# A new written-out order of 1,051 operations for a gated linear attention followed by a token and channel mixer

## The chip, the cores and the metric

One core of a Trainium2 chip. The metric is the time of one execution in device microseconds (us), lower is better. The kernel before took 176.54 us (median of 3 runs, 176.35 to 176.94).

## The reference

Four batches, 8 heads, 768 steps, 48 columns a head. An attention with a decaying state is computed first, and its output, 384 columns wide, goes through a two-part mixer:

```
f = 1 / (1 + exp(-f_logit))
for t in range(S):
    state = f[t] * state + outer(k[t], v[t])
    y[t]  = q[t] @ state
x  = y, heads side by side                      # 4 x 768 x 384
u  = x + (relu(x.T @ w_tok1) @ w_tok2).T        # mixes the 768 steps, through 256
out = u + relu(u @ w_ch1) @ w_ch2               # mixes the 384 columns, through 1536
```

## The kernel before

Everything runs in bf16 matmuls with float32 sums. The 768 steps of a batch are six chunks of 128. The kernel first builds a plan: some 1,051 small operations, each with a number in the order in which it was added, the engines that may run it, what it needs and makes, and the PSUM bank that it fills. `Plan.run` then issues them in the order of a list written out by hand of a program, `ORDER`. A token of the list is an operation's number; a letter after it (A, D, G) chooses ScalarE, VectorE or GpSimd where there is a choice; digits after colons are the PSUM banks (eight of them) that it takes; `z11` and `s18` at the head are idle matmuls of 512 and of 64 columns that only keep TensorE running. Every engine works through its own part of the list strictly in order and waits on semaphores for what an operation needs, so the list sets what each engine does next, but no times. GpSimd issues the loads, SyncE issues the stores, small copies and the transposes done by DMA, each in the list's order.

Operations are named here by kind, batch, chunk (or part). Those that the text speaks of:

- load,f / load,q / load,k / load,v (line 266, GpSimd; the first three of f on SyncE) and the loads of weights (line 272). For batch 0 a load brings two chunks, later one chunk; f of batches 1 to 3 comes in one load.
- gates: exp and ln of f on ScalarE (lines 371, 372; 388, 392 for batch 0), and lo (lines 379, 401), the low bf16 half of the logarithm, on VectorE or GpSimd.
- sums (lines 461, 462; 615, 618): a triangular matmul that adds the logarithms up along a chunk. G and Gi (lines 471, 473; 628, 630) are its exponentials, and gated (lines 490, 637) multiplies q and k by them on VectorE. grow and glast (lines 477, 481) bring the decay of a whole chunk to all partitions, by a small DMA from SyncE.
- turn: q and k of a chunk are transposed, by matmul and a copy (turned) in batches 0 to 2, by a DMA transpose from SyncE (line 503) in batch 3. The transposed chunk goes into one of two buffers, chunk number modulo 2, so that turn,3,3 must wait until y,3,1 has read its buffer.
- scores (lines 413, 676), masked (lines 541, 706, VectorE), parts (lines 429, 665: the chunk's share of the state), tsum, state and spread (the state's step and its copy into bf16, on VectorE, GpSimd and ScalarE), y (lines 560, 564, 743; within for pairs of batch 0, line 719) and its copies x_bf and x_nat.
- tok1, h1T, tok2, u, u_bf: the mixer over steps (tok1 is line 757, tok2 line 773, u line 789). ut transposes u: by matmul with a copy uT (line 811) in batches 0 and 1, by two DMA transposes (line 802) in batches 2 and 3, where ut,2,0 carries chunks 0 to 2 and ut,2,1 chunks 3 to 5.
- ch1 (line 826), zT (lines 357, 359), ch2 (line 845), sum (line 851, VectorE) and store (line 855, SyncE): the mixer over columns. ch1 and ch2 are over half of TensorE's time. ch1,b,th,cc is one of 24 pieces a batch, th the half of the steps; ch2,b,tt,0,k0 is a third of the sum of chunk tt.

The list weaves the batches into each other: while TensorE works on the mixer of batch b, the gates, sums, scores and states of batch b+1 are fed in between. In batch 0 the attention runs alone at the start, with chunks taken in pairs.

In the plan each operation carries a cost (`kind`). `run` does not read it; such costs serve the program that made the list.

## Time and profile before

| what | value |
|---|---|
| median of the runs shown | 176.54 us |
| the profiled execution | 175.49 us, with a span of 173.6 us from its first to its last instruction |
| TensorE busy | 162.2 us, 93% of the span |
| VectorE, ScalarE, GpSimd busy | 127.7, 101.4 and 92.6 us |
| moved from and to memory | 25.17 MB read, 4.72 MB written |
| loads issued by GpSimd | 56, those of 96 KB landing 5.1 (v) to 7.4 us (k) after their issue at the median, those of 1152 KB after 9.9 |
| DMA transposes | 6 of q and k, 4 of u, 3.3 and 2.9 us to landing at the median |

The page of the profile shows one execution. Its busy rows give how long each engine worked; a chain of waits, followed back from the last instruction, tells what set the end; timelines of one engine list its instructions in order of time, merged when they follow each other, with the idle time ahead of them in brackets and what ended it. "issue" there means that the engine waited for nothing that the profile shows. Matmuls overlap each other, so a row of 12 matmuls of 384 columns with a mean of 326 ns lasts far less than 12 times that.

### The profile page before, as it was taken

The numbers are of one execution on the slowest core, as the hardware profiler recorded it, in microseconds if no ns is written. First come the engines' busy times: TensorE is split into PE (matmuls) and PEld (weight loads), VectorE is DVE, ScalarE is ACT, GpSimd is POOL, SyncE is SP. The second block draws the span as 40 slices with busy tenths as digits, with TensorE's granted clock in tenths as the row PEclk, the third lists the DMA queues.
The fourth block names the chain that finished last, engine by engine and source line by source line (L and its number), as shares of the span: only waits on it lengthen the run. The fifth ranks groups of instructions, "written<-read, shape, count | busy, mean of one in ns | idle before, by whom it ended". The sixth has DMA issues, their size and how long they took to land.

```text
span 173.6 us, 4462 instructions
## 1 busy us (share of the span) xinstructions
PE 162.2 (93%) x1761; PEld 103.6 (60%) x1761; DVE 127.7 (74%) x272; ACT 101.4 (58%) x226; POOL 92.6 (53%) x135
## 2 busy tenths in 40 slices
PE   6998779999999999899999999896999999999990
PEld 2575655666566666566767665563656556656660
DVE  5778988969969857887999779895884804766141
ACT  3899896986681448799999547478457120032000
POOL 8999979994996998794983707321110020000000
PEclk9999978999999999999999999999999999999999
DMA  5999999999999999169999992967530151030075
GB/s 152 227 171 195 206 196 188 185 149 203 146 177 201 102 69 88 5 65 228 121 95 144 120 59 51 210 169 240 134 66 4 47 135 46 4 136 0 30 263 211
DMA packets 89573, 22.74 MB, mean 131 GB/s; under 512 B 82288, under 2 KB 88736, under 8 KB 89552
## 3 DMA queue, kind: packets, MB, share of 16 engines
q0 software_dynamic: 69600, 13.77, 91.2%
q1 hardware_dynamic: 19952, 8.69, 18.9%
q8 instruction: 14, 0.23, 0.6%
q14 instruction: 7, 0.06, 0.1%
HBM read 25.17 MB, written 4.72 MB: 172 GB/s over the span
## 4 chain that ended last, share of the span: by engine, by line
PE 83%; DVE 6%; DMA 5%; issue 3%; ACT 2%; DVEq 0%; ACTq 0%
PE ps L826 26%; PE ps L845 23%; PE ps L757 5%; DMA qkT<-qk 5%; PE ps L773 4%; PE ps L877 3%; PE ps L500 3%; PE ps L618 2%; PE ps L413 2%; PE ps L461 2%; PE ps L564 2%; PE ps L462 2%; PE ps L560 1%; DVE AmT L541 1%; PE ps L644 1%
## 5 line engine op out<-in xcount | busy, mean ns | idle before, releaser
L826 PE MATMUL ps<-uT,w_ch 128*128 128x384 bf16 x288 | 53.0, 326 | 0.1
L845 PE MATMUL ps<-w_ch,zT 128*128 128x384 bf16 (+2 forms) x300 | 52.6, 320 | 0.0
L845 PEld LDWEIGHTS <-zT 128*128 128x128 bf16 x300 | 28.2, 98 | 17.3
L826 PEld LDWEIGHTS <-w_ch 128*128 128x128 bf16 x288 | 27.2, 97 | 17.1 <-issue 0.3
L357 ACT ACTIVATE zT<-ps 128x384 bf16<-128x384 f32 x50 | 22.6, 496 | 24.8 <-DVE zT L359 12.6
L359 DVE TENSOR_SCALAR zT<-ps 128x384 bf16<-128x384 f32 x46 | 23.8, 549 | 6.9 <-PE ps L826 6.7
L851 DVE TENSOR_TENSOR x_nat<-x_nat,ps 128x384 f32<-128x384 f32 (+2 forms) x25 | 12.9, 530 | 16.2 <-PE ps L845 16.2
L541 DVE TENSOR_TENSOR AmT<-ps,tri_bf 128x512 bf16<-128x512 f32 x36 | 23.1, 682 | 2.0 <-PE ps L413 2.0
L266 POOL DMA_DIRECT2D v_sb<-in_v_dram x16 | 15.7, 984 | 3.4 <-DVE zT L359 3.4
L281 POOL CAST state_bd<-state 48x192 bf16<-48x192 f32 x27 | 9.2, 341 | 13.5 <-DVE state L549 4.3
L266 POOL DMA_DIRECT2D qk_sb<-in_q_dram x16 | 16.0, 1001 | 0.3 <-issue 0.2
L266 POOL DMA_DIRECT2D qk_sb<-in_k_dram x16 | 15.7, 990 | 0.1
L281 POOL CAST u_bf<-x_nat 128x384 bf16<-128x384 f32 x14 | 7.5, 548 | 14.5 <-issue 11.8
L789 DVE TENSOR_TENSOR x_nat<-x_nat,ps 128x384 f32<-128x384 f32 x21 | 10.8, 545 | 2.7 <-PE ps L773 2.6
L379 POOL TENSOR_TENSOR Llo<-L 128x384 bf16<-128x384 f32 x11 | 9.0, 825 | 6.4 <-ACT L L372 6.2
L757 PE MATMUL ps<-x_bf,w_tok 128*128 128x384 bf16 x48 | 12.0, 339 | 0.0
L490 DVE TENSOR_TENSOR qk<-qk_sb,GG 128x768 bf16<-128x768 bf16 x18 | 10.8, 620 | 0.7 <-DMA qkT<-qk 0.7
L277 ACT ACTIVATE x_bf<-ps 128x384 bf16<-128x384 f32 x14 | 6.9, 491 | 6.2 <-PE ps L564 6.2
L473 ACT ACTIVATE GG<-ps 128x384 bf16<-128x384 f32 x18 | 8.8, 497 | 2.3 <-PE ps L462 2.2
L471 ACT ACTIVATE GG<-ps 128x384 bf16<-128x384 f32 x18 | 8.6, 505 | 1.4 <-PE ps L462 0.9
L773 PE MATMUL ps<-h1T,w_tok 128*128 128x384 bf16 x48 | 9.3, 326 | 0.0
L577 POOL TENSOR_TENSOR state<-tsum,glast 128x192 f32<-128x192 f32 x9 | 4.7, 523 | 8.3 <-ACT state_bd L277 6.7
(100 smaller groups left out, 265.7 us busy)
## 6 DMA issues: line engine op xcount, KB each, us to landing
out_dram<-x_nat SPq DMA_DIRECT2D x23, 192.0 KB, 2.2
f_sb<-in_f_logit_dram POOLq DMA_DIRECT2D x3, 1152.0 KB, 9.9
f_sb<-in_f_logit_dram SPq DMA_DIRECT2D x3, 384.0 KB, 4.0
qk_sb<-in_q_dram POOLq DMA_DIRECT2D x12, 96.0 KB, 5.6
qk_sb<-in_k_dram POOLq DMA_DIRECT2D x12, 96.0 KB, 7.4
w_ch<-in_moe_w_ch_dram POOLq DMA_DIRECT2D x2, 576.0 KB, 9.3
v_sb<-in_v_dram POOLq DMA_DIRECT2D x12, 96.0 KB, 5.1
w_ch<-in_moe_w_ch_dram POOLq DMA_DIRECT2D x1, 1152.0 KB, 10.6
```

The costliest lines, as they stand in the source:

```text
L266: lambda eng=eng, into=into, of=of: eng.dma_start(out=into, in_=of),
L281: nc.gpsimd.tensor_copy(out_, in_)
L357: nc.scalar.activation(out_, in_, AF.Relu, bias=0.0, scale=1.0)
L359: nc.vector.tensor_scalar(out_, in_, 0.0, None, ALU.max)
L490: add(("gated", b, c, *names), DVE, lambda n=n: nc.vector.tensor_tensor(qk[it][:, n, :, 0:D], qk_sb[nb][:, n, :, c, :], GG[i][:, n], ALU.m ...
L541: add(("masked", b, c, p), DVE, lambda half=half, made=made: nc.vector.tensor_tensor(half, made(), tb4, ALU.mult), need=["tri_bf"], make=[ ...
L757: add(("tok1", b, rt, kt), PE, lambda rt=rt, kt=kt, pm=pm: nc.tensor.matmul(banks[pm.at][:, 0:DM], lhsT=w_tok1[:, kt, rt * 128:(rt + 1) * ...
L773: nc.tensor.matmul(banks[pm.at][:, 0:DM], lhsT=w_tok2[:, kt, tt * 128:(tt + 1) * 128], rhs=h1T[:, kt, :], start=(kt == 0 and not held), st ...
L789: nc.vector.tensor_tensor(to, un, banks[pm.at][:, 0:DM], ALU.add)
L826: nc.tensor.matmul(banks[pm.at][:, 0:384].rearrange("p (n t) -> p n t", t=128), lhsT=w[:, kt, c0:c0 + 128], rhs=uT[:, rows3, kt, :], start ...
L845: nc.tensor.matmul(banks[pm.at][:, 0:n1 - n0], lhsT=zT[:, kt, tt * 128:(tt + 1) * 128], rhs=w_ch2[:, kt, n0:n1], start=(kt == 0), stop=(kt ...
L851: add(("sum", b, tt, n0), DVE, lambda un=un, pm=pm, n=n1 - n0: nc.vector.tensor_tensor(un, un, banks[pm.at][:, 0:n], ALU.add), make=[("x_n ...
```

## The change

`ORDER` is replaced as a whole; nothing else in the file differs. It is a permutation of the same 1,051 operations with other choices of engine and of banks, and with ten idle matmuls of 512 columns and 22 of 64 at its head instead of eleven and 18.

```diff
 ORDER = """
-z11 s18 14D 6D 7G 8G 32 21G 9G 12D 33 0G 5G 1 10G 2 49 51 50 20G 15D 3D 17D 23D 24D 26D 27D 36 54 34 55 35 37 29D 18D 38
-22D 28 25D 53G 39 52D 19D 58 11G 13D 105:0 106 107 40 57D 56D 100:1 137:2 41 142:3 109 30D 102 101 103 108 59 111:0 104
...
+z10 s22 0G 20G 5G 7D 14G 6D 19D 21D 22G 1 13G 23A 2 26A 32 33 25G 8G 11D 34 3A 49 17D 28 35 36 51 53D 50 54 52D 55 24D
+15G 37 12G 39 105:0 58 9D 27D 16D 38 100:1 18D 57D 29D 30D 10G 31D 107 56G 108 106 110 109 102 142:2 101 104 103 137:0
+59 42 41 4G 40 61D 60D 114:1 119:3:4 115 111:5 144 139 145 138 112 175:0 62 143 125 113A 140 146 126G 116D 148:2 149
...
```

Told by names, what changes where the text goes on:

- The eight paired loads of batch 0 (two chunks each). Before: q,0,0 k,0,0 v,0,0 k,0,2 q,0,2 v,0,2 k,0,4 q,0,4. After: k,0,0 q,0,0 v,0,0 q,0,2 k,0,2 q,0,4 k,0,4 v,0,2. Then load,f,1 and load,v,0,4 in both.
- TensorE's opening. Before: sums of chunks 1, 0, 2, 3, the turns of chunks 0 and 1, with parts,0,0 ahead of the last, sums,0,5, ... sums,0,4, ... parts,0,2, within,0,0. After: sums 1, 0, 3, 2, turn,0,0 of k, parts,0,0, the other turns, sums,0,4, ... sums,0,5, ... parts,0,2, within,0,0. From there to within,0,2 and on to tok1 the two orders are nearly the same.
- Engines. 28 of the zT move from VectorE to ScalarE and 20 the other way. Seven lo move from GpSimd to VectorE and two the other way: 16 on VectorE and 8 on GpSimd after, 11 and 13 before. 11 spread move from ScalarE to GpSimd and 9 the other way; 7 x_bf and 7 x_nat move from ScalarE to VectorE, 5 and 3 the other way.
- Batch 3 on TensorE. Before: y,2,5, 22 operations that end with three ch2, scores,3,1, scores,3,0, parts,3,2, sums,3,4, ch1,2 (four), y,3,1, ch1,2 (six), y,3,0, sums,3,5, scores,3,2, scores,3,3. After: y,2,5, 20 operations, scores,3,0, scores,3,1, parts,3,2, two ch2, y,3,0, sums,3,5, sums,3,4, three ch2, y,3,1, ch1,2 (seven), scores,3,2, scores,3,3.
- SyncE around it. Before: glast,3,0, turn,3,0, turn,3,1, ut,2,0, ut,2,1, glast,3,2, turn,3,2, glast,3,3, store,0,3, store,0,1, turn,3,3, glast,3,4, six stores. After: glast,3,0, turn,3,1, turn,3,0, glast,3,3, glast,3,2, store,0,0, store,1,0, glast,3,1, ut,2,0, ut,2,1, store,0,1, turn,3,2, turn,3,3, store,0,2, glast,3,4.
- GpSimd in the middle. After: spread,1,0, load,f,2, load,k,2,0, load,v,2,1, lo,1,5, load,q,2,0, load,k,2,1, both halves of spread,1,1.
- The stores on SyncE at the end. Before: ... 3,3, 2,1, 1,4, 2,4, 1,0, 1,5, 3,2, the right part of 3,5, the left one, 3,1, 3,4, 3,0. After: ... 1,4, 2,4, 3,3, the right part of 3,5, 3,4, 3,2, 3,1, the left part of 3,5, 3,0, with all of batches 1 and 2 ahead of 3,3. The last seven TensorE operations are the same in both.

More of the change, by code (lines that the diff above doesn't have):

```diff
@@ new lines @@
+962G 967 994:3 1008:2 970:4 971A 977A 998:6 806 792 817 968:0 972:4 996:1 991A 802 992:5 995D 993A 1000:3 1001D 988:7
+568 563 973A 1009A 969A 1010:5 982:3 1004:0 984:2 978:4 989D 997A 1002:1 1005A 986:0 999D 983A 1012:3 573 1006:6 987D
+1011A 1003A 797 1014:0 1026:1 1036:5 979D 980:4 1046:7 807 1015A 985D 1007D 1021:0 1041:6 981A 1042 1031:4 1047 1013D
+1037 1032 1048 1049 1027 1033 1028 1043 1034 578 1016:4 812 1044 1029 1038 1022 1023 1035 1050 1039 1024 1017 1040 1018
+1030 1025 1045 1019 1020
```

76 lines of the change are left out of this document (35 added, 41 removed).

## Prediction

> **What bounds the kernel now.** I read the page first, its busy rows and the chain that ended last.
>
> ```profile
> span 173.6 us, 4462 instructions
> ...
> PE 162.2 (93%) x1761; PEld 103.6 (60%) x1761; DVE 127.7 (74%) x272; ACT 101.4 (58%) x226; POOL 92.6 (53%) x135
> ...
> q8 instruction: 14, 0.23, 0.6%
> ...
> PE 83%; DVE 6%; DMA 5%; issue 3%; ACT 2%; DVEq 0%; ACTq 0%
> ```
>
> TensorE is the bound, and the new list has the same matmuls, three more idle ones apart. So the time can only change where TensorE stands, or where its clock is low. Next I cut the span into stages (columns: length, busy time and instructions of each engine, granted clock, DMA share, GB/s).
>
> ```profile
> 7.26:23.32 16.06, 13.04 (x325) 9.60 (x322) 13.91 (x35) 14.65 (x32) 15.46 (x21) 1.00 1.60 189
> 23.32:33.66 10.34, 10.34 (x146) 7.16 (x146) 8.79 (x20) 8.53 (x20) 9.04 (x15) 0.83 1.60 192
> 33.66:111.00 77.34, 76.36 (x800) 49.32 (x797) 64.13 (x126) 55.09 (x126) 56.75 (x73) 1.00 1.55 122
> 111.00:121.00 10.00, 8.14 (x104) 5.03 (x106) 8.12 (x17) 7.39 (x18) 1.59 (x5) 1.00 0.76 197
> 121.00:169.50 48.50, 48.49 (x368) 30.06 (x366) 27.34 (x55) 11.35 (x26) 3.04 (x7) 1.00 0.28 84
> ```
>
> The first row is the opening, batch 0's attention: TensorE idles 16.06 - 13.04 = 3.0 us. It idles 1.0 in the long middle, 1.9 between 111 and 121, and nothing from there to 169.5. The second stage runs at 0.83 of the clock, which is 0.17 x 10.34 = 1.8 us of a lower clock's loss. That is all a list can win, with some 4 us at the end that no matmul fills. Dense work goes at 0.163 us a matmul of 384 columns, in the chain by time:
>
> ```profile
> 137.55 5.20 PE ps L845 x32
> ```
>
> **The transposes of batch 3.** Two entries of the chain are DMAs, and TensorE's and SyncE's timelines show what surrounds them.
>
> ```profile
> 107.69 3.28 DMA qkT<-qk
> 115.65 4.93 DMA qkT<-qk
> ```
>
> ```profile
> 108.51 2.12 PE L845 MATMUL ps<-w_ch,zT 128*128 128x384 bf16 x12
> 111.02 0.62 PE L413 MATMUL ps<-qkT 48*128 48x128 bf16 x16 [0.39 <-DMA qkT<-qk]
> ...
> 111.95 0.34 PE L461 MATMUL ps<-L,tri_bf 128*128 128x384 bf16 x1
> ...
> 112.57 2.11 PE L826 MATMUL ps<-uT,w_ch 128*128 128x384 bf16 x12
> ...
> 114.75 0.36 PE L564 MATMUL ps<-v_sb,AmT 128*128 128x48 bf16 x8
> ...
> 118.51 0.40 PE L413 MATMUL ps<-qkT 48*128 48x128 bf16 x8
> 120.63 0.40 PE L413 MATMUL ps<-qkT 48*128 48x128 bf16 x8 [1.73 <-DMA qkT<-qk]
> ```
>
> ```profile
> 112.54 1.26 SPq L503 DMA_TRANSPOSE qkT<-qk  x1
> ...
> 114.48 1.06 SPq L855 DMA_DIRECT2D out_dram<-x_nat  x2
> 115.65 1.24 SPq L503 DMA_TRANSPOSE qkT<-qk  x1
> ```
>
> Three losses, from start to start. scores,3,1 begins at 111.02, where the 12 matmuls before it end at 108.51 + 12 x 0.163 = 110.46: 0.55. sums,3,4 and the first product of ch1,2 lie 0.62 apart where two matmuls of 384 columns need 0.33: 0.29. scores,3,3 begins 2.12 after scores,3,2, whose 8 matmuls take half of the 0.55 of a 16-matmul pair: 1.8. Together 2.65.
>
> In the new list turn,3,1, which is issued first, waits for y,2,5, the last reader of its buffer. Between y,2,5 and scores,3,0 stand 49 matmuls of 384 columns, 8.0 us, against the issue of one transpose (1.26) and the transfer of the next (3.28), 4.6 us: the 0.55 goes. Late next would be gated,3,0, which has the rest, 3.4 us, as its cover. ch1,2 no longer follows sums,3,4 at once, so the 0.29 goes. turn,3,3 must wait for y,3,1 in both lists, since it overwrites that chunk's buffer. Before, y,3,1 was done at 114.75 + 0.36 = 115.11, but SyncE was issuing two stores until 115.54. After, turn,3,2 stands right ahead of turn,3,3, and one store ahead of both, so I expect the issue at y,3,1's end. Seven ch1 (21 x 0.163 = 3.42) and scores,3,2 (0.3) follow until scores,3,3: 3.7 us of cover for a transfer of 3.28, if it isn't slowed to 4.93 again. I take no wait: the 1.8 goes.
>
> SyncE issues in order, so a step that waits there holds all behind it. store,0,0,0, store,1,0,0 and glast,3,1 now stand ahead of ut,2,0 and ut,2,1. The matmuls of those two sums end over 20 operations before, so the stores only cost their issue, twice half of the 1.06 above. ut,2,1 needs u,2,5 and u_bf,2,5, some 0.55 each as a vector row further down shows, and about 3.3 for the transfer, 4.4 us. From tok2,2,5 to ch1,2,1,11, its first user, stand 24 matmuls of 384 columns (3.9 us) and the scores, parts and y of chunks 0 and 1 (0.55 for the scores alone), so about 5 us: hidden by a little, and if that cover is gone, ch1,2 and all behind it start so much later.
>
> **The opening.** Three of the loads around which the list is reordered, v,0,2, q,0,4 and f,1, as GpSimd issues them, and the views of the DMAs issued at those moments (last column: us from issue to landing):
>
> ```profile
> 8.49 0.88 POOL L266 DMA_DIRECT2D v_sb<-in_v_dram  x1
> ...
> 10.22 0.90 POOL L266 DMA_DIRECT2D qk_sb<-in_q_dram  x1
> ...
> 12.41 2.26 POOL L266 DMA_DIRECT2D f_sb<-in_f_logit_dram  x1
> ```
>
> ```profile
> v_sb<-in_v_dram POOLq DMA_DIRECT2D x1, 192.0 KB, 5.1
> ...
> qk_sb<-in_q_dram POOLq DMA_DIRECT2D x1, 192.0 KB, 6.8
> ...
> f_sb<-in_f_logit_dram POOLq DMA_DIRECT2D x1, 1152.0 KB, 9.9
> ```
>
> ```profile
> 17.12 0.24 PE L665 MATMUL ps<-v_sb,qk 64*64 64x48 bf16 x7 [0.41 <-issue]
> ...
> 22.38 0.22 PE L719 MATMUL ps<-v_sb,zT 64*128 64x48 bf16 x4 [0.57 <-ACT x_bf L277]
> 23.32 0.51 PE L719 MATMUL ps<-v_sb,zT 64*128 64x48 bf16 x27 [0.72 <-issue]
> ```
>
> TensorE stands twice inside an operation, for nothing but "issue": at the 222nd and the 350th matmul, 128 apart. A load and a matmul are two instructions, so that is each 256 instructions. Queue q8 moved 0.23 MB in 14 transfers, 16 KB each, and 2 x 1761 instructions over 14 are 252. I read these as fetches of TensorE's own instructions, late because the loads fill the DMA engines. By count of the new list the same two places fall into the same two operations, parts,0,2 and within,0,2. The second begins to wait for its block when the first is passed (17.12), and has it 6.2 us later.
>
> v,0,2 moves from the sixth to the eighth of these loads: it lands not at 13.6 but about where the eighth did, 10.22 + 6.8 = 17.0. parts,0,2 needs it and ran from 16.3, standing until 17.12: cost 0.1 while the fetch covers it. What starts earlier in the new list (one idle matmul of 512 columns fewer, four small ones more, both low parts of the first sums on VectorE) shortens what lies ahead of 17.12, where fetch and load hold TensorE anyway: I count it at nothing. So within,0,2 again goes on at 23.3, and the low clock follows, since TensorE has stood at the same places before. Bounds: 1.3 gained (0.41, and 0.94 from 22.38 to 23.32) if the fetches come sooner; 5.2 lost if v,0,2 lands only with f,1 (12.41 + 9.9 = 22.3 against 17.1); and the 1.8 of the clock, gone or doubled. I stay near the row of the eighth load.
>
> The Trainium skill ("Runtime: NRT & Kernel Launch", Instruction fetch mechanics) says that blocks of 256 instructions are fetched ahead and the crossing is mostly hidden. The block size agrees with the rows; "hidden" does not, with 0.41 and 0.72 of standing. By that rule the opening would move with its data, the fourth rival.
>
> **What VectorE gets.** Low parts (lo) on VectorE rise from 11 to 16, on GpSimd they fall from 13 to 8.
>
> ```profile
> L379 DVE TENSOR_TENSOR Llo<-L 128x384 bf16<-128x384 f32 x7 | 5.0, 721 | 0.0
> ...
> L789 DVE TENSOR_TENSOR x_nat<-x_nat,ps 128x384 f32<-128x384 f32 x21 | 10.8, 545 | 2.7 <-PE ps L773 2.6
> ```
>
> ```profile
> 68.56 1.50 DVE L379 TENSOR_TENSOR Llo<-L 128x384 bf16<-128x384 f32 x1
> ```
>
> ```profile
> 68.34 0.84 POOL L379 TENSOR_TENSOR Llo<-L 128x384 bf16<-128x384 f32 x1
> ```
>
> ```profile
> 69.41 0.49 PE L773 MATMUL ps<-h1T,w_tok 128*128 128x384 bf16 x2
> 70.37 0.33 PE L461 MATMUL ps<-L,tri_bf 128*128 128x384 bf16 x1 [0.48 <-DVE uT L279]
> ```
>
> lo,2,0 took 1.50 instead of 0.72 while GpSimd ran lo,2,1, and TensorE then lost 70.37 - 69.41 - 0.33 = 0.63. The new list has lo,2,1 on VectorE just as GpSimd has lo,2,2, so I keep this loss. The new list has tight places of its own. ut,0,4 takes the bank of tok2,0,0,1, which u_bf,0,0 and u,0,0 (0.55 each) must empty, with uT,0,2 between them (a third operation, some 0.35 as an estimate, being a shorter copy); TensorE has seven matmuls of 128 to 384 columns and turn,1,1 meanwhile, about 1.3: 0.2 lost. ch2,1,3,0,0 takes the bank of tok2,2,5 after two scores and parts, under 1.0, and u,2,5 must empty it behind two gatings and a sum: 0 to 1 lost, 0.5 taken. y,1,2 needs both halves of spread,1,1 from GpSimd, where f,2 (2.26), four loads of 0.9 and a low part (0.84) stand ahead of them, 6.7 us after state,1,0; 43 matmuls of 384 columns (7.0 us) and smaller ones cover that: nothing lost, and each us that GpSimd is behind is one at y,1,2. Five more low parts beside GpSimd cost nothing to 5 x 0.78 = 3.9; each has the sums of its chunk as its only reader, which the list puts a few operations later, so I take nothing beyond the 0.63, with 3.9 as the upper end.
>
> The Trainium skill ("SBUF — State Buffer", SBUF: two separate sides) says that a VectorE operation with two inputs in SBUF and a GpSimd operation that reads SBUF exclude each other. The 1.50 agrees. By that rule each of the five can wait out a GpSimd operation, 5 x 0.84 = 4.2 as an estimate, and the second rival would be the outcome.
>
> **The end.**
>
> ```profile
> 164.62 6.39 SPq L855 DMA_DIRECT2D out_dram<-x_nat  x10
> ```
>
> ```profile
> 169.59 0.55 DVE L851 TENSOR_TENSOR x_nat<-x_nat,ps 128x384 f32<-128x384 f32 x1 [0.35 <-PE ps L845]
> ```
>
> ```profile
> 170.60 0.41 SPq L855 DMA_DIRECT2D out_dram<-x_nat  x1
> ```
>
> The last sum is done at 170.14; its store waits 0.46 because SyncE still works off ten stores. In the new list the sums of batches 1 and 2 are all done before the first ch2 of batch 3, their stores are issued ahead of store,3,3, and the last seven TensorE operations are the same as before. So SyncE is free when the last sum is done: I take 0.4. If it is not, nothing changes here, since the 0.46 stands already.
>
> **Sum.** 0.55 + 0.29 + 1.8 + 0.4 = 3.0 gained, 0.1 + 0.2 + 0.5 = 0.8 lost, 2.2 net. The profiled execution took 175.49 (span 173.6), which gives 173.3. The runs shown have a median of 176.54, 1.05 above it, and the new kernel will be timed as they were; against that it is 176.54 - 2.2 = **174.3**.
>
> **Rivals.** 1. *turn,3,3 is slowed again.* By the count of 128 matmuls a fetch falls at y,3,0 in the old list and at scores,3,2 in the new one; if it meets the transfer, 4.93 against 3.7 leaves 1.2: 175.5. For it: nearly the same place. Against: one store behind it, not six. 2. *The low parts fill VectorE*: 2.2 of the 3.9 reach TensorE, no change: 176.5. For it: the 1.50 and the 0.63. Against: the six other low parts of that row had 5.0 - 1.5 = 3.5 us, 0.58 each, so most met no GpSimd operation. 3. *Slower: v,0,2 is late.* From 17.1 on each us of its landing is one of the total; from 17.1 + 2.2 + 0.5 = 19.8 the kernel is slower. Landing at 21 costs 3.9: 178.2. For it: the eighth load already took 6.8, and f,1 is issued right behind. Against: loads so far landed in their order. 4. *The opening isn't held by fetches*: 1.3 more, 173.0. For it: parts,0,0 has its inputs earlier. Against: the two rows with "issue".
>
> **How the numbers follow.** Forecast 0.36, slowed transpose 0.18, full VectorE 0.16, late load 0.19, free opening 0.11. A measurement here tells 0.3% (0.5 us) from no change. Faster: 0.36 + 0.18 + 0.11 = 0.65; same 0.16; slower 0.19. The range 172.3 to 177.7 leaves out the worse half of the late load, a lower clock that stays longer, and the ends of the free opening.
>
> **What would show it.** Right: no wait on qkT at scores,3,1 and scores,3,3, a last store issued within 0.1 of its sum, and issue stalls in parts,0,2 and within,0,2 with the latter going on near 23.3. Wrong: parts,0,2 waiting for v_sb after 17.2; a turn,3,3 near 5 us; new waits of TensorE on VectorE between 34 and 111.

## The result, and the profile after

The new list is slower: 178.75 us (median of 4 runs, 177.81 to 178.96) against 176.56 for the kernel before (4 runs, 176.35 to 176.94), a ratio of 1.0111, 95% interval 1.0072 to 1.0151. The forecast was 174.3, and 178.75 lies outside its range too. The profiled execution took 178.96, with a span of 177.2, 3.6 more than before.

The page of the kernel after, with the rows that answer to those of before:

```profile
span 177.2 us, 4472 instructions
...
PE 163.1 (92%) x1764; PEld 104.1 (59%) x1764; DVE 132.1 (75%) x272; ACT 102.6 (58%) x229; POOL 89.7 (51%) x132
...
q8 instruction: 13, 0.21, 0.5%
...
PE 51%; DMA 19%; POOL 16%; issue 6%; DVE 4%; ACT 1%; POOLq 0%; DVEq 0%
```

TensorE has as much to do as before, and VectorE 4.4 us more. The chain that ended last tells more than the busy rows: before, 83% of it was TensorE, now only 51%, and DMAs, which had 5%, and GpSimd, which had no entry in this line, have 35%. The same stages (columns as in the prediction):

```profile
7.26:23.32 16.06, 12.63 (x316) 9.17 (x313) 15.64 (x37) 14.22 (x30) 14.70 (x20) 1.00 1.61 187
23.32:33.66 10.34, 9.57 (x136) 6.44 (x137) 8.67 (x16) 8.28 (x20) 9.32 (x14) 0.83 1.70 187
33.66:111.00 77.34, 73.57 (x783) 47.61 (x781) 66.01 (x132) 56.57 (x130) 52.95 (x66) 1.00 1.58 128
111.00:121.00 10.00, 9.94 (x104) 6.34 (x103) 9.14 (x19) 3.75 (x10) 3.42 (x7) 1.00 0.68 161
121.00:173.00 52.00, 51.01 (x396) 31.67 (x394) 28.37 (x58) 14.83 (x35) 3.44 (x8) 1.00 0.26 79
```

The stage from 111 to 121 is full now, as forecast. But the long middle, where TensorE idled 1.0, idles 3.8. What it waits for, in the list of TensorE's waits (us in total, times, longest):

```profile
PE ps L560 <- POOL state_bd L281: 1.9, 3, 0.8
...
PE ps L461 <- DVE x_nat L789: 1.1, 1, 1.1
PE ps L719 <- issue: 1.0, 1, 1.0
PE ps L413 <- DMA qkT<-qk: 1.0, 1, 1.0
PE ps L615 <- POOL Llo L401: 0.9, 1, 0.9
```

Of these lines only the third and the fourth were there before, with 0.7 and 2.1.

To add up where the time went I lined each TensorE operation up with the time at which it would have begun if all operations from ch1,0,0,5 on had taken their usual time in dense work (the median of their kind in the trace of before). Where the lag behind that grows, TensorE lost time. ch1,0,0,5 is the first product behind the opening; it begins at 33.66 before and 34.65 after.

| stage | forecast | measured |
|---|---|---|
| opening, to ch1,0,0,5 | +0.1 | +0.98 |
| from there to 111 | +0.7 | +4.5 (lag 6.3 after, 1.8 before) |
| 111 to the last matmul | -2.6 | -1.5 (1.4 after, 2.9 before) |
| tail | -0.4 | -0.42 |
| sum | -2.2 | +3.6 |

The 4.5 of the middle are y,1,1 0.61, y,1,2 0.93, tok1,1,0,2 0.53, y,1,4 0.16, y,1,5 0.82 (3.05 together), sums,2,1 1.25 where before lost 0.76 at sums,2,0 and 2,1, ut,1,0 0.54, and smaller ones. tok1,1,0,2 belongs to them at second hand: state,1,2 came late on GpSimd (55.31), spread,1,2 waited for it on ScalarE, and x_bf,1,2, which tok1 reads, stood behind that.

### The profile page after: what moved, and what is told of

Read it like the earlier page. It is cut to its first block, busy times and chain, and to the rows that moved or that the text cites. A ratio compares the mean times of both kernels' runs of the same rounds, so it can differ in the third digit from the quotient of the medians.

```text
span 177.2 us, 4472 instructions
## 1 busy us (share of the span) xinstructions
PE 163.1 (92%) x1764; PEld 104.1 (59%) x1764; DVE 132.1 (75%) x272; ACT 102.6 (58%) x229; POOL 89.7 (51%) x132
## 4 chain that ended last, share of the span: by engine, by line
PE 51%; DMA 19%; POOL 16%; issue 6%; DVE 4%; ACT 1%; POOLq 0%; DVEq 0%
PE ps L845 22%; PE ps L826 16%; DMA w_ch<-in_moe_w_ch_dram 10%; DMA f_sb<-in_f_logit_dram 6%; POOL qk_sb L266 6%; PE ps L773 3%; DMA qkT<-qk 3%; POOL v_sb L266 3%; PE ps L757 3%; POOL state_bd L281 2%; PE ps L413 2%; DVE x_nat L789 1%; PE ps L564 1%; POOL u_bf L281 1%; PE ps L560 1%
## 5 line engine op out<-in xcount | busy, mean ns | idle before, releaser
L826 PE MATMUL ps<-uT,w_ch 128*128 128x384 bf16 x288 | 52.4, 326 | 0.1
L357 ACT ACTIVATE zT<-ps 128x384 bf16<-128x384 f32 x58 | 26.3, 496 | 28.4 <-PE ps L826 28.2
L359 DVE TENSOR_SCALAR zT<-ps 128x384 bf16<-128x384 f32 x38 | 19.4, 549 | 8.3 <-PE ps L826 5.9
L541 DVE TENSOR_TENSOR AmT<-ps,tri_bf 128x512 bf16<-128x512 f32 x36 | 23.3, 681 | 0.4 <-PE ps L413 0.2
L281 POOL CAST state_bd<-state 48x192 bf16<-48x192 f32 x29 | 11.9, 411 | 18.1 <-DVE state L577 11.9
L281 POOL CAST u_bf<-x_nat 128x384 bf16<-128x384 f32 x11 | 6.3, 593 | 22.1 <-DVE x_nat L789 13.1
L773 PE MATMUL ps<-h1T,w_tok 128*128 128x384 bf16 x48 | 9.9, 326 | 0.0
L277 ACT ACTIVATE x_bf<-ps 128x384 bf16<-128x384 f32 x12 | 5.8, 485 | 7.0 <-PE ps L564 3.9
L371 ACT ACTIVATE f_sb<-f_sb 128x384 f32<-128x384 f32 x18 | 8.9, 528 | 0.8 <-DMA f_sb<-in_f_logit_dram 0.7
L372 ACT ACTIVATE L<-f_sb 128x384 f32<-128x384 f32 x18 | 9.1, 523 | 0.1
```

The lines of the kernel that those rows point to most:

```text
L281: nc.gpsimd.tensor_copy(out_, in_)
L357: nc.scalar.activation(out_, in_, AF.Relu, bias=0.0, scale=1.0)
L359: nc.vector.tensor_scalar(out_, in_, 0.0, None, ALU.max)
L541: add(("masked", b, c, p), DVE, lambda half=half, made=made: nc.vector.tensor_tensor(half, made(), tb4, ALU.mult), need=["tri_bf"], make=[ ...
L773: nc.tensor.matmul(banks[pm.at][:, 0:DM], lhsT=w_tok2[:, kt, tt * 128:(tt + 1) * 128], rhs=h1T[:, kt, :], start=(kt == 0 and not held), st ...
L826: nc.tensor.matmul(banks[pm.at][:, 0:384].rearrange("p (n t) -> p n t", t=128), lhsT=w[:, kt, c0:c0 + 128], rhs=uT[:, rows3, kt, :], start ...
```

## What holds GpSimd back

Two timelines of the kernel after, GpSimd's and TensorE's, over that middle (the brackets hold the idle time ahead and what ended it):

```profile
38.10 1.01 POOL L272 DMA_DIRECT2D w_ch<-in_moe_w_ch_dram  x1 [1.32 <-DMA w_ch<-in_moe_w_ch_dram]
...
43.37 1.82 POOL L266 DMA_DIRECT2D v_sb<-in_v_dram  x2
...
48.50 0.87 POOL L266 DMA_DIRECT2D qk_sb<-in_k_dram  x1 [0.76 <-DMA w_ch<-in_moe_w_ch_dram]
...
52.87 0.72 POOL L281 CAST state_bd<-state 48x192 bf16<-48x192 f32 x2
...
59.08 0.87 POOL L266 DMA_DIRECT2D qk_sb<-in_k_dram  x1 [1.95 <-DMA f_sb<-in_f_logit_dram]
60.01 0.50 POOL L577 TENSOR_TENSOR state<-tsum,glast 128x192 f32<-128x192 f32 x1
```

```profile
53.64 0.33 PE L560 MATMUL ps<-state_bd,qkT 128*128 128x96 bf16 x4 [0.76 <-POOL state_bd L281]
```

A load that is issued on GpSimd stands there and waits for another load to land: k,2,3 at 59.08 for f,2, which was issued at 45.51 and took 13.3 us:

```profile
f_sb<-in_f_logit_dram POOLq DMA_DIRECT2D x1, 1152.0 KB, 13.3
```

k,2,3 doesn't read f,2. It is the 42nd load of GpSimd, f,2 the 34th; k,2,0 is the 35th and waits for w_ch2, the 27th; w_ch2 waits for the second half of w_ch1, the 19th. In the program as it was built every load from the ninth on has a wait on one of eight semaphores, taken in turn, which the load eight places before sets when it lands: a wait of this program, which says nothing of the chip. GpSimd works in order, so state,1,3 and all the state work behind it stands until 60.01, and y,1,4 and y,1,5 wait. In the kernel before, the same 34th and 42nd load were some 15 us apart, and f,2 took 9.7.

Theory A, then: the loads ahead of the state work, each holding GpSimd 0.9 us, and the wait for the load eight places before cost the 3.05. Rival B: VectorE, which has five more low parts, sets the pace of the middle, and GpSimd's waits only stand in front of it.

## The experiments

The kernel before ran beside each, and its own runs spread from 173.6 to 178.0, so small differences are read in the traces. The granted clock of the stretch from 23.32 to 33.66 comes out at 0.83 in some executions and near 0.67 in others, of the kernel before's opening and of the kernel after's. These are averages: the records of the clock show it at 0.50 for 3.4 us (24.1 to 27.5 in the kernel before, 25.8 to 29.2 in a_beside) or for 6.8 us (24.1 to 30.9 in a_z14), and at 1.00 around that. a_beside and a_z14, alike up to 22.5, have ch1,0,0,5 1.0 apart, so its start is compared at like clocks. "Lag behind it" is the time that TensorE loses from ch1,0,0,5 to its last matmul, counted as above; the clock ahead of ch1,0,0,5 isn't in it.

| kernel | ratio to before, 95% interval | ch1,0,0,5 at, clock | lag behind it |
|---|---|---|---|
| before | 1 | 33.66, 0.83 | 4.7 |
| after | 1.0111 (1.0072 to 1.0151) | 34.65, 0.83 | 7.7 |
| a_again | 1.0109 (1.005 to 1.0167) | 34.47, 0.83 | 6.9 |
| a_tiny | 1.0219 (1.0061 to 1.0377) | 35.50, 0.67 | 6.5 |
| a_mid | 0.9989 (0.9936 to 1.0041) | 35.89, 0.67 | 5.2 |
| b_loads | 1.0045 (1.0007 to 1.0083) | 35.18, 0.68 | 5.1 |
| a_beside | 1.0079 (1.0037 to 1.0121) | 34.88, 0.83 | 5.0 |
| a_z14 | 1.0085 (1.0053 to 1.0117) | 35.87, 0.67 | 5.5 |
| a_best1 | 0.9995 (0.9962 to 1.0027) | 34.78, 0.83 | 4.5 |
| b_z14 | 0.998 (0.9933 to 1.0028) | 36.25, 0.67 | 4.2 |
| b_s47 | 1.0024 (0.9989 to 1.006) | 33.70, 0.83 | 5.3 |
| b_s47x | 1.002 (0.9976 to 1.0063) | 34.43, 0.72 | 5.0 |
| a_head | 1.0148 (1.0065 to 1.0231) | 35.68, 0.69 | 5.4 |
| a_dve | 1.0131 (1.0053 to 1.0209) | 35.44, 0.67 | 6.7 |
| a_open | 1.0191 (1.0055 to 1.0326) | 36.13, 0.67 | 5.4 |
| a_s90 | 1.0138 (1.0054 to 1.0222) | 35.14, 0.69 | 5.8 |
| g230 | 1.0115 (1.0052 to 1.0179) | 37.32, 0.67 | 3.4 |
| g230m | 1.0104 (1.0028 to 1.018) | 37.53, 0.68 | 5.1 |
| g523, g523z | 1.0452, 1.0448 (1.0393 to 1.0511) | 34.08, 33.94, 0.83 | 13.0 |

a_again is the kernel after once more. It came out at 1.0109, close to the 1.0111 of the first measurement; its lag is 0.7 smaller, mostly since y,1,1 and y,1,2 waited less.

> The changed kernel once more, unaltered, on the chip of the three runs that follow, since the kernel before spread there from 174.7 to 177.8 us. Every theory expects 1.0 to 1.5 per cent above the kernel before, and in the trace the same places: y,1,1 to y,1,5 waiting for state_bd, scores,3,3 for a turn,3,3 of near 4.9 us if a fetch starts within it, within,0,2 standing for 1.0 to 1.5.

**a_mid: GpSimd's order.** Only GpSimd's own order is changed:

```diff
-lo,1,4 v,1,4 v,1,5 spread,1,0 f,2 k,2,0 v,2,1 lo,1,5 q,2,0 k,2,1 spread,1,1 spread,1,1 k,2,2 k,2,5 state,1,2
-spread,1,2 q,2,1 k,2,3 state,1,3 v,2,0 spread,1,3 q,2,2 spread,1,3 state,1,4 v,2,3 spread,1,4 q,2,3
+lo,1,4 spread,1,0 v,1,4 v,1,5 f,2 lo,1,5 spread,1,1 spread,1,1 k,2,0 v,2,1 q,2,0 state,1,2 spread,1,2 k,2,1 k,2,2
+k,2,5 q,2,1 state,1,3 spread,1,3 spread,1,3 k,2,3 state,1,4 spread,1,4 v,2,0 q,2,2 v,2,3 q,2,3
```

> The changed kernel with GpSimd's own order alone mended between 42 and 65 us: the state work (spread,1,0, spread,1,1, state and spread,1,2, 1,3 and 1,4) stands ahead of the loads behind which it stood; every load is still there, five to eight places later at most. Theory A (a load on GpSimd waits until the load eight places before it has landed, GpSimd works in order, so the state work behind a held load is late and y,1,1 to y,1,5 wait: 0.61 + 0.93 + 0.53 + 0.16 + 0.82 = 3.05 us): the waits of the y lines on state_bd fall from 1.9 us to under 0.4, and the time falls by 2.2 to 3.0 us, to 175.8 to 176.6. Rival B (VectorE, with five more low parts, sets the pace of this stretch; the waits on GpSimd only stand in front of it): the waits move to masked, tsum or x_bf on VectorE, and the time falls by less than 1 us, to 177.8 or more.

No y line waits on state_bd any more; y,1,1, y,1,4 and y,1,5 on TensorE's timeline of a_mid carry no bracket:

```profile
46.25 0.33 PE L560 MATMUL ps<-state_bd,qkT 128*128 128x96 bf16 x4
...
62.48 0.33 PE L560 MATMUL ps<-state_bd,qkT 128*128 128x96 bf16 x4
...
63.50 0.33 PE L560 MATMUL ps<-state_bd,qkT 128*128 128x96 bf16 x4
```

The lag falls by 2.4 against the kernel after and by 1.7 against a_again, the ratio by 1.2 per cent, about 2.1 us, a little less than expected; its interval doesn't touch that of a_again. Theory A holds. Of the 3.05, 0.58 came back at ch1,0,1,3, and ut of batch 1 lost 1.75 in place of 0.54: rival B has a small part of it.

**a_tiny: what counts.** One small load more, behind f,2:

```diff
-... 391:1 81 378 407 ...
+... 391:1 81 1051 378 407 ...
+    add(("tiny",), POOL, lambda: nc.gpsimd.dma_start(out=tiny, in_=moe_w_tok1[0:1, 0:64]))
```

> The changed kernel with one more load on GpSimd, of 64 numbers of the first weights that nobody uses, just behind load f,2,0; nothing else is moved. Theory A in its strict form (load n waits for load n-8, whatever their sizes): every later load is one further on, so the small one, not k,2,0, waits for w_ch2, and q,2,1, not k,2,3, waits for f,2,0: q,2,1 is issued 0.3 after f,2,0 has landed, near 59 us, 2.5 to 3 us after spread,1,2, and k,2,3 follows it without a wait of its own. Rival K (what is full is room for bytes or for packets: one small load fills none): k,2,3 still waits, q,2,1 is issued at once behind spread,1,2 as before.

GpSimd's timeline of a_tiny:

```profile
48.17 0.52 POOL L874 DMA_DIRECT2D tiny<-in_moe_w_tok_dram  x1 [0.87 <-DMA w_ch<-in_moe_w_ch_dram]
...
59.03 0.94 POOL L266 DMA_DIRECT2D qk_sb<-in_q_dram  x1 [2.19 <-DMA f_sb<-in_f_logit_dram]
59.97 0.88 POOL L266 DMA_DIRECT2D qk_sb<-in_k_dram  x1
```

The waits moved one load on: the small one stood for w_ch2, q,2,1 stood for f,2, and k,2,3 followed without a wait. What counts is the place in the row of loads, not the bytes. The time, 1.0219 (1.0061 to 1.0377), isn't told from that of the kernel after.

**b_loads: the same cause put into the kernel before.**

```diff
-f,2 state,1,1 spread,1,1 spread,1,1 k,2,1 q,2,3 state,1,2 k,2,5 q,2,1 v,2,3 state,1,3 spread,1,3 spread,1,3 q,2,0 q,2,2
+f,2 k,2,1 q,2,3 k,2,5 state,1,1 spread,1,1 spread,1,1 q,2,1 v,2,3 state,1,2 q,2,0 q,2,2 v,2,5 state,1,3 spread,1,3 spread,1,3
```

> The kernel before, with nothing changed but GpSimd's order between 47 and 66 us: eight of its loads are put ahead of the state work, so that the 42nd load (v,2,5) is issued just ahead of state,1,3 and must wait for the 34th (f,2,0; landed 57.31 in the kernel before, later with more loads beside it). Theory A (the load eight places on waits, and GpSimd in order makes the state work late): v,2,5 waits until 0.3 to 0.5 after f,2,0 has landed, near 58 to 60; state,1,3 starts at 59 to 61 in place of 57.85, y,1,4 and y,1,5 wait for state_bd, and the time rises by 1 to 2.5 us over the kernel before. Rival B (VectorE sets the pace of that stretch): within 0.4 us of the kernel before.

Slower, by 0.45 per cent, but less than expected and not in the way expected: v,2,5 was issued at 59.57 without a wait, since f,2 had landed. What came late was state,1,2, at 57.17 and not 54.55, behind three loads of 0.9 each, and y,1,3 lost 0.85. So the issue of loads holds the state work even where no wait does; in these traces the long waits came where the load eight places ahead was a large one that landed late.

**a_beside: a low part beside GpSimd.** In the kernel after lo,2,1 and GpSimd's work at that time, in the timelines of VectorE and GpSimd:

```profile
71.05 1.92 DVE L379 TENSOR_TENSOR Llo<-L 128x384 bf16<-128x384 f32 x1
```

```profile
70.44 1.66 POOL L379 TENSOR_TENSOR Llo<-L 128x384 bf16<-128x384 f32 x2
```

```diff
-lo,2,4 lo,2,2 u_bf,1,3 q,2,4 u_bf,1,5 u_bf,1,2 u_bf,1,0 k,3,0 v,2,5 v,2,4
+q,2,4 v,2,5 lo,2,2 lo,2,4 u_bf,1,3 u_bf,1,5 u_bf,1,2 u_bf,1,0 k,3,0 v,2,4
```

> The changed kernel with two loads (q,2,4 and v,2,5) moved ahead of GpSimd's lo,2,2, lo,2,4 and u_bf,1,3 at 70 us, so that VectorE's lo,2,1 runs beside the issue of loads and no longer beside GpSimd's arithmetic; lo,2,1 itself, its engine and its place on VectorE are unchanged. Theory E (lo,2,1 took 1.91 us in place of 0.55 because GpSimd's arithmetic ran beside it): lo,2,1 takes 0.5 to 0.8, u,1,1 ends 1.1 us sooner, and the 1.08 us wait of sums,2,1 for it falls under 0.3; the time falls by 0.5 to 1.2 us, to 177.5 to 178.2, unless sums,2,2, whose lo,2,2 is now 1.8 us later, takes it back. Rival F (lo,2,1 is slow for another reason, as its operands' place): it stays at 1.7 to 2.0 and the time at 178.4 to 179.

VectorE's timeline of a_beside, lo,2,1:

```profile
70.50 0.89 DVE L379 TENSOR_TENSOR Llo<-L 128x384 bf16<-128x384 f32 x1
```

It took 0.89, and the lag at sums,2,1 fell from 1.25 to 0.22; ut of batch 1 gave 0.5 of that back. The time, 1.0079, isn't told from that of the kernel after. Theory E holds in direction, but not quite in size: beside two loads the same operation took 0.89 here, 1.23 in a_mid and 1.16 in a_best1, while other low parts beside loads took 0.55. And lo,2,3, now beside four u_bf, took 1.60: the collision was moved. What the loads' issue does to it isn't settled. Nor does each low part beside another lose: in the opening of the kernel after lo,0,3 took 0.56 on VectorE (8.59) beside lo,0,2 on GpSimd, and there it was lo,0,2 that took long, 1.14.

**a_z14: the fetch beside turn,3,3.** In the kernel after turn,3,3 was issued at 118.40 and took 4.86, in the chain by time:

```profile
118.40 4.86 DMA qkT<-qk
```

Queue q8, the instruction fetches, moved a packet of 16 KB at 121.2 to 122.1; the view of the DMAs over 120.9 to 122.3 has it:

```profile
q8 instruction: 1, 0.02, 4.1%
```

```diff
-z10 s22 0G 20G ...
+z14 0G 20G ...
```

> The changed kernel with 14 idle matmuls at its head in place of 10 wide and 22 narrow ones: 18 matmuls fewer ahead of the work, so TensorE's instruction fetches (one in 128 matmuls) come 18 matmuls later in the work; nothing else is changed. Theory G (turn,3,3 takes 4.85 us in place of 3.1 to 3.3 because a fetch at 121.0 to 121.9 shares its DMA engines): that fetch comes 1.5 to 1.9 us later, after turn,3,3 has landed, turn,3,3 takes 3.1 to 3.4, the 1.07 us wait of scores,3,3 is gone, and the time falls by about 1 us, to 177.5 to 178.0, if the opening does not change by the shift of its own fetches. Rival H (turn,3,3 is slow for what SP's queue or the loads do): it stays at 4.7 to 5 us and the time within 0.4 of 178.75.

The fetch came at 123.2, turn,3,3 took 3.06, and scores,3,3 no longer waits: scores,3,2 and scores,3,3 are one row on TensorE's timeline of a_z14:

```profile
122.11 0.62 PE L413 MATMUL ps<-qkT 48*128 48x128 bf16 x16
```

Theory G holds; the time, 1.0085, isn't told from 1.0111. In the 20 traces turn,3,0 and turn,3,3 are 40 transposes. 18 took 4.25 to 4.95, and in each of them a fetch began, between 0.1 us ahead of the issue and 2.9 after it; the other 22 took 3.05 to 3.34. In four of the 22 a fetch began too, in their last 0.5: at 2.66, 2.67, 2.72 and 3.05 us. Near the end it isn't certain, then, since fetches at 2.70 and 2.72 made the same transpose take 4.76 and 4.77 in a_again and a_mid. Nor does each transpose suffer so much: in a_s90 a fetch met ut,2,1 (3.20), turn,3,4 (3.06) and turn,3,5 (3.49). What decides is open.

**b_z14, b_s47, b_s47x: is the 1.8 to be had in the kernel before?** Its fetch came at 118.5, where turn,3,3 (issued at 115.65) would have landed at 118.7 to 118.9.

b_z14:

```diff
-z11 s18 14D 6D ...
+z14 s4 14D 6D ...
```

> The kernel before with 14 wide and 4 narrow idle matmuls at its head in place of 11 and 18: 11 matmuls fewer, so that the fetch at 118.5, which began 0.2 us before turn,3,3 would have landed, comes about 1 us later. Theory G (that fetch is all that made turn,3,3 take 4.93): turn,3,3 takes 3.0 to 3.4, the 1.81 us wait of scores,3,3 falls under 0.3, and the time falls by 1.5 to 1.8 us below the kernel before, 0.990 to 0.992 of it, which is what the prediction counted for this wait. Rival H: it stays at 4.9 and the time within 0.3 per cent.

turn,3,3 took 3.06 and its wait was gone. But ScalarE's timeline of b_z14 shows what was late next:

```profile
126.89 0.49 ACT L277 ACTIVATE x_nat<-ps 128x384 f32<-128x384 f32 x1 [1.31 <-DMA out_dram<-x_nat]
```

The fetch now lay at 122.2 to 123.2 beside the six stores, whose median landing went from 2.8 to 4.1 (in b_s47 below, where no fetch begins among them, it was 2.0). x_nat,3,0 overwrites what one of them sends and waited 1.31; ch1,2,1,5 and ch1,2,0,4 lost 0.38 and 1.00. Of 1.81 only 0.4 was left, and the time is not told from that of before.

b_s47, with the fetch on the other side:

```diff
-z11 s18 14D 6D ...
+z7 s47 14D 6D ...
```

> The kernel before with 7 wide and 47 narrow idle matmuls at its head in place of 11 and 18, 25 more, so that the fetch that began at 118.5, 0.2 us before turn,3,3 would have landed, comes 2.5 us sooner, near 116, beside the first half of turn,3,3 (issued 115.65) and ahead of the six stores from 117.57 on. The shift by 11 the other way (b_z14) freed turn,3,3 but put the fetch among the stores, and x_nat,3,0 waited 1.31 us for one of them. Theory G (a fetch harms the transfer in whose last part it begins): turn,3,3 takes 3.0 to 3.4, the stores land in 2.8 as in the kernel before, scores,3,3 waits under 0.3 and ch1,2,1,5 not at all; 1.5 to 1.8 us below the kernel before, ratio 0.990 to 0.992. Rival Q (any fetch beside a transposing transfer lengthens it): turn,3,3 stays at 4.5 to 5 and the time within 0.4 us of the kernel before.

Rival Q is right here: the fetch began at 116.5, turn,3,3 was issued at 116.60 and took 4.55, its issue alone 2.76 on SyncE's timeline of b_s47:

```profile
116.60 2.76 SPq L503 DMA_TRANSPOSE qkT<-qk  x1
```

The two stores issued just ahead, at 115.43 and 116.08, took 4.18 and 4.02, where in the kernel before they took 2.08 and 1.95. The six stores behind, which had the fetch among them in b_z14, are free of it here, in the views of the DMAs of b_z14 (120.1 to 123.7) and of b_s47 (120 to 123):

```profile
out_dram<-x_nat SPq DMA_DIRECT2D x6, 192.0 KB, 4.1
```

```profile
out_dram<-x_nat SPq DMA_DIRECT2D x6, 192.0 KB, 2.0
```

So here the fetch lengthened the two stores as well as the transpose. scores,3,2 and scores,3,3 lost 1.66 of the 1.81; another 0.9 went at sums,3,1 and just behind it, which the kernel before doesn't lose and which stays unexplained.

b_s47x, the same with scores,3,1 (851) behind scores,3,0 (850) and parts,3,2 (886):

```diff
-... 851:0:2 873 880 882 850:7:3 886:6 855 ...
+... 873 880 882 850:7:3 886:6 851:0:2 855 ...
```

> As b_s47, with one more change on TensorE: scores,3,1 stands behind scores,3,0 and parts,3,2 and no longer ahead of them, so that turn,3,1's last 0.5 us lie beside them. This is the 0.55 us that the prediction counted for scores,3,1. If that wait was on the path, 0.4 to 0.6 us below b_s47; if scores,3,3 or the stores take it up, within 0.2 of it.

The wait of scores,3,1 stayed (0.58 of lag), so this run says nothing on whether the terms add.

**a_head, a_dve, a_open, a_s90: the opening.**

a_head, GpSimd's order (lo,0,2 goes to VectorE, with lo,0,3 ahead of grow1):

```diff
-tri0 inc2 L0p kh1 half20 tri qh1 half21 Llo1p k,0,0 q,0,0 grow0 v,0,0 kh0 q,0,2 k,0,2 Llo2p lo,0,2 q,0,4 k,0,4 ones_bf v,0,2
+tri0 inc2 L0p kh1 tri qh1 k,0,0 q,0,0 half20 half21 Llo1p v,0,0 q,0,2 k,0,2 v,0,2 kh0 q,0,4 k,0,4 Llo2p grow0 ones_bf
```

> The changed kernel with GpSimd's opening alone mended: the first load is issued ahead of the memsets that waited for VectorE's half2 (before's first load was issued at 2.66, after's at 3.19), v,0,2 is the sixth load again and not the eighth, and lo,0,2 is on VectorE beside lo,0,3. Theory C (the opening lost its 0.98 us to these three): parts,0,2 starts at 16.3 to 16.8 in place of 17.66, the 0.9 us wait for lo,0,2 is gone, and ch1,0,0,5 starts 0.6 to 1.0 earlier than the changed kernel's 34.65; time 177.8 to 178.2. Rival D (the instruction fetch of TensorE sets when within,0,2 goes on, and it lies behind the same transfers as now): parts,0,2 is early, but the issue stall in within,0,2 grows by as much, and ch1,0,0,5 is within 0.3 of 34.65; time 178.5 or more.

a_dve, VectorE's order; a_open is both:

```diff
-... grow2 exc2 lo,0,1 lo,0,0 pmask00 L2p pmask01 grow1 sbd0 lo,0,3 pmask1 pmask10 pmask11 gated,0,1 ...
+... exc2 pmask00 pmask01 pmask1 pmask10 pmask11 lo,0,1 lo,0,0 L2p lo,0,3 sbd0 gated,0,1 ...
```

> The changed kernel with VectorE's own order alone mended up to 14 us: the masks and memsets of the set-up stand in its idle time between 3.8 and 5.6 us or behind 24.7, no longer ahead of gated,0,1,k (ready at 9.25 at the latest, run at 10.73), and turned,0,0,k stands ahead of gated,0,2,q and gated,0,3,q (it was ready at 12.78 and ran at 13.80). Theory I (VectorE's order is what the opening lost): parts,0,0 starts at 11.2 to 11.8 in place of 12.02, scores,0,0 at 13.3 to 13.9 in place of 14.53, within,0,0 0.5 to 0.9 sooner than 18.23, and ch1,0,0,5 0.5 to 1.0 sooner than in the unaltered kernel at the same granted clock; time 0.5 to 1.0 below it. Rival D (the fetch in within,0,2 sets it): within,0,2 starts sooner and stands longer; ch1,0,0,5 within 0.3. Rival J (lo,0,2 on GpSimd, at 9.83, and v,0,2, at 17.6, set it and not VectorE): parts,0,2 still starts at 17.6.

> The changed kernel with both parts of the opening mended, GpSimd's (first load sooner, v,0,2 sixth, lo,0,2 on VectorE) and VectorE's (masks in its idle time, turned,0,0,k ahead of gated,0,2,q). Theory L (each alone only uncovered the other): parts,0,0 at 11.0 to 11.7, parts,0,2 at 16.2 to 16.8, within,0,2 starts 0.8 to 1.2 sooner than 22.52. Rival D (the fetch sets when within,0,2 goes on): it starts that much sooner and ends where it did, at 24.4 to 24.6, and the time is that of the unaltered kernel within 0.5.

a_s90:

```diff
-z10 s22 0G 20G ...
+z2 s90 0G 20G ...
```

> The changed kernel with 2 wide and 90 narrow idle matmuls at its head in place of 10 and 22: 60 matmuls more, so that TensorE comes to each fetch 60 matmuls sooner in the work: the one that stood in within,0,2 falls near scores,0,2. Theory D (TensorE's fetch, which comes late behind the loads, is what holds the opening): the stall moves to another line, and ch1,0,0,5 comes at another time, 0.5 us or more sooner or later than 34.5 to 34.7 at the granted clock of 0.83. Theory I (VectorE's chain of masked sets it): within,0,2 runs in one piece from 22.5 to 23.6, but within,0,4 still starts at 25.0 or later behind masked,0,5,0 (ready at 24.74), and ch1,0,0,5 gains 0.3 to 0.7.

TensorE's timelines of the kernel after and of a_s90, within,0,2 and what follows:

```profile
23.74 0.73 PE L719 MATMUL ps<-v_sb,zT 64*128 64x48 bf16 x29 [1.02 <-issue]
24.39 0.82 PE L743 MATMUL ps<-state_bd,zT 128*128 128x96 bf16 x8
```

```profile
22.63 0.74 PE L719 MATMUL ps<-v_sb,zT 64*128 64x48 bf16 x32 [0.35 <-ACT x_bf L277]
23.31 0.82 PE L743 MATMUL ps<-state_bd,zT 128*128 128x96 bf16 x8
...
25.93 0.54 PE L719 MATMUL ps<-v_sb,zT 64*128 64x48 bf16 x17 [0.67 <-issue]
```

And parts,0,2 in the kernel after and in a_s90:

```profile
17.66 0.44 PE L665 MATMUL ps<-v_sb,qk 64*64 64x48 bf16 x32 [0.23 <-DMA v_sb<-in_v_dram]
```

```profile
17.63 0.44 PE L665 MATMUL ps<-v_sb,qk 64*64 64x48 bf16 x32 [0.20 <-DVE zT L706]
```

Mending the orders won little. In a_head the sums were through 0.4 sooner, and yet parts,0,0 came 0.36 later and parts,0,2 at 17.99. a_dve brought within,0,2 0.35 sooner, but it stood 1.3 and was passed at 24.48, as in the kernel after (24.46). a_open had parts,0,0 at 11.71, then waited for G and Gi on ScalarE, stood 1.35 in within,0,2 and passed it at 25.01. Theories C and L are wrong; of theory I the part that VectorE sets parts,0,2 is right, as the last rows show, but not that a few operations out of its way win the time. In a_s90 the fetch left within,0,2, which ran in one piece, and stood in within,0,4 for 0.67; y,0,3 began 1.1 sooner, y,0,4 (26.40 for 26.45) not. ch1,0,0,5 came at 35.14, 0.7 sooner than a_mid and a_z14 at nearly their clock; the time isn't told apart. So theory D holds as far as these traces go: the block that TensorE waits for sets when within,0,2 goes on, and it came 0.4 later than before (23.74 for 23.32).

Why later can be read from the rows, though no run tried it by itself. In the 17 traces in which TensorE stood in within,0,2 it went on 5.8 to 6.5 us after it had passed the end of the block before (a block of 256 instructions, 128 matmuls with their weight loads). That end lies in or just behind parts,0,2, and TensorE passed it at 17.12 before (6.2 us) and at 17.81 after (5.9 us). parts,0,2 was late: in the new list it takes the bank that masked,0,0,0 empties on VectorE, done at 17.57, just as v,0,2 landed (17.61). In a_s90 v,0,2 was there at 16.71, in a_head and a_open at 14.3, and parts,0,2 still began within 0.1 us of the end of masked,0,0,0 (17.63, 17.99, 17.93). So it was the bank and VectorE's order, and not the load.

Of the other 0.6 of the 0.98, 0.35 is a wait of sums,1,1 for lo,1,1, one of the low parts moved to VectorE, which took 1.84 (26.16 to 28.00) beside GpSimd's lo,1,0:

```profile
28.05 0.32 PE L462 MATMUL ps<-Llo,tri_bf 128*128 128x384 bf16 x1 [0.35 <-DVE Llo L379]
```

The rest stays open, and the 0.98 is a figure of the executions at 0.83: there the opening of before has ch1,0,0,5 at 33.7 to 34.1 and that of after at 34.5 to 34.9, while at 0.67 and 0.68 it comes at 36.25 (b_z14) and 35.18 (b_loads) with the first and at 35.87 and 35.89 (a_z14, a_mid) with the second, not told apart.

**g230, g230m, g523, g523z: two lists grafted.** The first 230 or 523 entries of before, then what is left in the order of after; g230m with a_mid's order and `z14`, g523z with `z14`.

> The kernel before's list for all engines up to u,0,5 (its first 230 entries, some 31 us), and the changed kernel's list for all that is left. Theory M (the 0.98 us of the opening lie in the lists up to there, as a whole, though mending GpSimd's part, VectorE's part or both won nothing): ch1,0,0,5 starts at 33.5 to 34.0 where the granted clock of the stretch from 23.32 to 33.66 is 0.83, and at 34.8 to 35.1 where it is 0.67 (the unaltered changed kernel: 34.5 to 34.7, and 35.4 to 35.9 in its variants); y,1,1 to y,1,5 wait for state_bd as before; time 0.6 to 1.2 below the changed kernel, 1.004 to 1.008 of the kernel before. Rival O (the opening's loss is one of the loads and fetches behind it and shows again later): ch1,0,0,5 as in the changed kernel, 1.010 to 1.012.

> The kernel before's list up to u,0,5, then the changed kernel's with GpSimd's state work ahead of its loads between 42 and 65 us, and 14 wide idle matmuls at the head. The three places lie one behind the other: 1.0 + 2.4 + 1.0 us below the changed kernel's 178.75, 174.0 to 174.8, ratio 0.986 to 0.992 of the kernel before. If the opening's part fails (rival O), 0.992 to 0.997.

> The kernel before's list up to its 523rd entry (some 70 us: the opening and the middle as they were), and the changed kernel's list for the rest. If opening and middle are all that the change lost, what is left of it is the gain that the prediction summed: 0.55 (scores,3,1) + 0.29 (ch1,2) + 0.4 (tail) = 1.2 us below the kernel before where a fetch still hits turn,3,3 (4.7 to 4.9 us), ratio 0.993; and 2.0 to 2.4 below, 0.986 to 0.989, where it misses. Rival P (what the late part wins is eaten by VectorE, which it keeps busier): within 0.3 per cent of the kernel before.

> As g523, with 14 wide idle matmuls at the head in place of 11 wide and 18 narrow, 15 fewer, so that the fetch near 121 comes 1.3 us later and turn,3,3 is through. Theory G: turn,3,3 3.0 to 3.3, no wait of scores,3,3; 0.55 + 0.29 + 1.81 + 0.4 = 3.05 us less than the kernel before at most, of which the kernel before with the same shift gave 1.4 back at ch1,2,1,5 and ch1,2,0,4; 1.7 to 3.0 below the kernel before, ratio 0.983 to 0.990. Rival P: 1 us or less below it.

These failed as tests, since the seam, where one list ends and the other begins, cost more than what they were to tell. In g230 ch1,0,0,5 comes 1.4 to 1.5 later than in a_mid and a_z14 at the same clock; in g230m another 1.3 are lost right behind the seam, where the granted clock is 0.50 from 36.8 to 40.2. In g523 parts,2,0 alone loses 2.9 and the stretch from 75 to 102 some 11, because some hundred operations that the list of after has done by then come late in it, and because the clock falls to 0.50 there from 79.4 to 86.2. They say nothing on the opening. One thing is seen by the way: in g230 the y lines don't wait at all (lag 3.4), though GpSimd's order is that of after: with TensorE 2 us later behind the same loads, the cover was enough. That fits theory A.

**a_best1: the mended parts together** (a_mid's order, a_beside's with u_bf,1,0 ahead of u_bf,1,2, and `z14`).

> Three mended parts together: GpSimd's state work ahead of its loads (42 to 65 us), two loads ahead of its lo,2,2 and lo,2,4 with u_bf,1,0 ahead of u_bf,1,2 (70 to 77 us), and 18 idle matmuls fewer at the head so that the fetch at 121 comes after turn,3,3. Theories A, E and G add up, since the three places lie one behind the other: 2.4 + 1.0 + 1.0 us below the unaltered kernel, 4 to 4.5 us, which is 1.5 to 2.5 us below the kernel before. If one of them only makes room for the next wait, the sum is smaller by that part: rival B 1.5 to 2.5 below the unaltered kernel, no more.

y and scores,3,3 wait no more, and the lag is 4.5, under the 4.7 of before; but u_bf,1,5, put last, held ut,1,5 for 1.06. That is 0.9995, level with the kernel before and some 2 us below the kernel after, half of the 4 to 4.5 that the three parts were to give: rival B's size. No version here is faster than the kernel before beyond its interval.

## Why the prediction was wrong, step by step

- **"43 matmuls of 384 columns (7.0 us) and smaller ones cover that: nothing lost", at y,1,2.** This step failed. It counted 6.7 us on GpSimd from state,1,0 on; from the end of state,1,0 (43.27) until both halves of spread,1,1 were done (53.59), 10.3 passed. Left out were v,1,4, v,1,5 and spread,1,0, which stand ahead of f,2 as well (2.2), that a load can wait itself (k,2,0 stood 0.76 for w_ch2), and the two copies (0.72). The cover was larger than 7.0 too, some 9.4 up to where y,1,2 would have begun (the 0.61 lost at y,1,1 among it), and y,1,2 lost the difference, 0.93. The same sum was not made for y,1,1, y,1,4 and y,1,5, where loads were moved ahead of state work in the same way and k,2,3 stood 1.95. The prediction named the price ("each us that GpSimd is behind is one at y,1,2") and then took zero. Together with tok1,1,0,2 that is 3.05, more than half of the 5.8 between forecast and result, and a_mid, which moves nothing but GpSimd's order, won most of it back. None of the four rivals was this one.
- **"I count it at nothing", for the opening.** Failed by 0.9. v,0,2 landed at 17.6, not 17.0, but masked,0,0,0 held parts,0,2 until 17.57 anyway, so rival 3's mechanism is not what happened. Of the two places where fetches were to hold TensorE, one did: it stood 1.02 in within,0,2, and not at all in parts,0,2. What failed is "fetch and load hold TensorE anyway" at 17.12: TensorE passed that place at 17.81, held by VectorE, so within,0,2 did not go on at 23.3 but at 23.74. That is 0.4; another 0.35 is the wait for lo,1,1, and the rest stays open. The Trainium skill ("Runtime: NRT & Kernel Launch", Instruction fetch mechanics) has the crossing of a block mostly hidden; a_s90 shows the stand moving with the count of matmuls, 1.02 in one operation, 0.67 in another, so it was not hidden here.
- **"I take no wait: the 1.8 goes", at scores,3,3.** Half right. The cover was there (turn,3,3 was issued at y,3,1's end and seven ch1 followed), but the transfer met a fetch and took 4.86, as rival 1 said with a cost of 1.2: 1.07 was left, 0.74 won. a_z14 shows that the rest is to be had in the new list; in the old one neither b_z14 nor b_s47 got it.
- **0.55 and 0.29.** Right: neither wait is there.
- **0.63 kept, and "nothing beyond" for five more low parts.** The mechanism was right, the size off: two of the 16 were slowed, lo,1,1 (1.84) and lo,2,1 (1.92), together 2.7 above 0.55 each, within the bound of 3.9. The first reached TensorE with 0.35, the second with 1.25, where 0.63 was kept. The Trainium skill ("SBUF — State Buffer", SBUF: two separate sides) has the two engines shut each other out; the 1.84 and 1.92 agree.
- **0.2 at ut,0,4 and 0.5 at ch2,1,3,0,0.** Not there; ut,1,0 (0.54) and ch1,1,0,8 (0.29) lost in their place, which no step had looked at.
- **The end, 0.4.** Right: the last sum was done at 174.16, the span ended 3.04 later in place of 3.46.

## What to carry to other kernels

When work moves behind loads on an in-order engine, sum not only the time of their issue but ask for each load which earlier one it waits for: here the one eight places before, and a large load there can hold everything behind it. Count from the operation that makes the data, and not from the first load that was moved. A gain that a profile shows at one DMA may belong to a neighbour in time, like an instruction fetch; move the neighbour by a few idle matmuls and see both whether the gain comes and what it hits next. Waits covered in one list are not covered in another, so each moved operation with a reader on the bound engine wants its own sum of time and cover.
